# Block attention and an FFN in one kernel: PV on four array quadrants, DMA transposes of x, a new order of loads and work

## The chip, the cores and the metric

The kernel runs on one core of a Trainium2 chip. TensorE (PE) does matmuls into PSUM, VectorE (DVE) and ScalarE (ACT) work on PSUM and SBUF, GpSimd (POOL) and SyncE (SP) issue the DMAs here. The metric is the device time of one execution in microseconds (us); less is better.

## What is computed

Attention inside chunks of 64 tokens, then a feed-forward network (FFN) with a swish of its own slope per hidden column:

```python
B, H, S, D = 8, 8, 576, 64                       # q, k, v: fp32
scores = q_c @ k_c.T / sqrt(D)                   # per chunk of 64 tokens and head
attn   = exp(scores - max) / sum(...)
x      = (attn @ v_c) as [B * S, H * D]          # 4608 x 512
h      = x @ w_in                                # 512 -> 2048
g      = h / (1 + exp(-beta * h))
out    = g @ w_out                               # 2048 -> 512, fp32
```

## The kernel before

The 4,608 tokens are cut into 18 units of 256 tokens (four chunks, two tiles of 128). The FFN takes them in blocks: units 0 and 1 alone, then pairs (2, 3), (4, 5) and so on, ten blocks.

Attention of a unit has these steps. `load_qk` and `load_v` bring q, k and v from POOL's DMA queue, cast to fp16. `emit_T` transposes k and q on DVE in 32 x 32 blocks, four instructions. `emit_sc` does 64 small score matmuls (32 rows of contraction, accumulated over two halves `e`) into two PSUM tiles `sc0`, `sc1`; ACT takes the exponential into `et`. `emit_pv` is called once per tile of 128 tokens: 16 matmuls of 64 x 64 x 65, chunk `c` on partitions 64c of both input and output, so on two diagonal quadrants of the PE array; the 65th column of v is 1.0 and gives the sum. DVE divides (`rd`, then `x16`). `emit_xt` turns the tile on PE (four transposes into PSUM `xp`, which shares its buffer with `sc0`) and DVE copies it to `xt`.

The FFN of a block j: for each of 16 hidden groups m, `emit_m` does four matmuls into `hps` (contraction 512), ACT takes tanh into `sg`, DVE forms `gt` in fp16 (named stt below). `emit_t` does 16 matmuls for a tile of 128 tokens into `ops`, ACT copies to `osb`, SP's queue stores it. `hps` and `ops` rotate over four PSUM buffers.

Each engine runs its instructions in program order; nothing reorders them. That order is written out by hand: attention of the next block is taken in steps (`attn_step`), one ahead of each of the four `emit_t` of the block before (at m = 4), so a scoring step stands between two output tiles; the xt of the block's last tile stands directly ahead of its first `hps`. Loads come from POOL in the order unit 0, a quarter of `w_in`, unit 1, the rest of `w_in`, unit 2, all of `w_out`, unit 3; later units as attention advances. Eight POOL DMAs can be in flight.

Of the kernel before, what the change touches and what calls it, by code (L numbers as in the profile page):

```python
# [8 lines left out]
FP32 = mybir.dt.float32  # L9
FP16 = mybir.dt.float16  # L10
ACTF = mybir.ActivationFunctionType
ALU = mybir.AluOpType
# [3 lines left out]
def kernel(  # L16
# [10 lines left out]
    nc = tc.nc  # L27
# [3 lines left out]
    CH = 64  # L31
# [10 lines left out]
    qk_p = ctx.enter_context(tc.tile_pool(name="qk", bufs=5))  # L42
    qt_p = ctx.enter_context(tc.tile_pool(name="qt", bufs=2))
    et_p = ctx.enter_context(tc.tile_pool(name="et", bufs=3))
    rd_p = ctx.enter_context(tc.tile_pool(name="rd", bufs=3))
    x_p = ctx.enter_context(tc.tile_pool(name="x", bufs=3))
    gt_p = ctx.enter_context(tc.tile_pool(name="gt", bufs=2))
    sg_p = ctx.enter_context(tc.tile_pool(name="sg", bufs=3))
    osb_p = ctx.enter_context(tc.tile_pool(name="osb", bufs=3))
# [5 lines left out]
    beta_sb = const.tile([128, KFF], FP32)  # L55
    beta2_sb = const.tile([128, KFF], FP32)
    w_in16 = big.tile([128, KDM, DFF], FP16)
    w_out16 = big.tile([128, KFF, DM], FP16)
    vbig = big.tile([128, NTILE, H, VP], FP16)

    blocks = []
    u0 = 0
    for n in [1, 1] + [2] * ((NU - 2) // 2):
        blocks.append((u0, n))
        u0 += n
    NB = len(blocks)
    xt_t = {}
    unit_block = {}
    for j, (u0, n) in enumerate(blocks):
        xt_t[j] = big.tile([128, KDM, n * UNIT], FP16, name=f"xt{j}")  # L70
        for u in range(u0, u0 + n):
            unit_block[u] = (j, u - u0)
# [28 lines left out]

    def load_w_in(g):
        n = DFF // 4
        nc.gpsimd.dma_start(  # L104
            out=w_in16[:, :, g * n:(g + 1) * n],
            in_=moe_w_in[:, g * n:(g + 1) * n].rearrange("(k p) f -> p k f", p=128),
        )

    def load_w_out(g):
        n = KFF // 4  # L110
        nc.gpsimd.dma_start(  # L111
            out=w_out16[:, g * n:(g + 1) * n, :],
            in_=moe_w_out[g * n * 128:(g + 1) * n * 128, :].rearrange("(k p) f -> p k f", p=128),
        )
# [4 lines left out]
    def emit_T(u):  # L119
        for src, dst, nm in ((k_t, kT, "kT"), (q_t, qT, "qT")):  # L120
            a = src.pop(u)
            t = qt_p.tile([128, H, 2, 32, 2], FP16, tag=nm, name=nm)
            for r in range(2):
                nc.vector.transpose(  # L124
                    out=t[:, :, :, :, r],
                    in_=a[:, :, r, :].rearrange("p h (e i) -> p h e i", e=2),
                )
            dst[u] = t

    et_t = {}  # L130

    def emit_sc(u):
        qt, kt = qT.pop(u), kT.pop(u)
        sc = [ps_s.tile([128, H, CH], FP32, tag=f"sc{s}", name=f"sc{s}") for s in range(2)]
        for h in range(H):
            for e in range(2):
                for c in range(4):
                    p0, o0 = 32 * c, 64 * (c % 2)
                    nc.tensor.matmul(  # L139
                        out=sc[c // 2][o0:o0 + 64, h, :],  # L140
                        lhsT=kt[p0:p0 + 32, h, e].rearrange("p i r -> p (i r)"),
                        rhs=qt[p0:p0 + 32, h, e].rearrange("p i r -> p (i r)"),
                        start=(e == 0),
                        stop=(e == 1),
                    )
        for s in range(2):
            et = et_p.tile([128, H, CH], FP16, tag=f"et{s}", name=f"et{s}")
            nc.scalar.activation(out=et, in_=sc[s], func=ACTF.Exp, scale=scale)
            et_t[u, s] = et

    def emit_pv(u, s):
        i = 2 * u + s
        et = et_t.pop((u, s))
        x = ps_x.tile([128, 2, 4, 128], FP32, tag="x", name="x")
        for h in range(H):
            for c in range(2):
                p0 = 64 * c
                nc.tensor.matmul(  # L158
                    out=x[p0:p0 + 64, h // 4, h % 4, 0:D + 1],
                    lhsT=et[p0:p0 + 64, h, :],  # L160
                    rhs=vbig[p0:p0 + 64, i, h, 0:D + 1],
                )
        rd = rd_p.tile([128, 2, 4, 1], FP32, tag="rd", name="rd")
        nc.vector.reciprocal(out=rd, in_=x[:, :, :, D:D + 1])  # L164
        x16 = x_p.tile([128, 2, 4, D], FP16, tag="x16", name="x16")
        nc.vector.tensor_tensor(
            out=x16, in0=x[:, :, :, 0:D], in1=rd.to_broadcast([128, 2, 4, D]), op=ALU.mult
        )
        j, o = unit_block[u]
        t0 = o * UNIT + s * 128  # L170
        pend_x.append((j, t0, x16))

    pend_x = []

    def emit_xt():
        j, t0, x16 = pend_x.pop()
        xp = ps_s.tile([128, KDM, 128], FP16, tag="sc0", name="xp")
        xf = x16.rearrange("p a h d -> p (a h d)")
        for g in range(KDM):
            nc.tensor.transpose(out=xp[:, g, :], in_=xf[:, g * 128:(g + 1) * 128], identity=ident)  # L180
        nc.vector.tensor_copy(out=xt_t[j][:, :, t0:t0 + 128], in_=xp)  # L181
# [3 lines left out]
    def emit_m(j, m):  # L185
        n = blocks[j][1] * UNIT
        if m == 0:
            gt_t[j] = gt_p.tile([128, KFF, n], FP16, tag="gt", name="gt")
        hps = ps_p.tile([128, n], FP32, tag="p", name="hps")
        for kk in range(KDM):  # L190
            nc.tensor.matmul(  # L191
                out=hps,
                lhsT=w_in16[:, kk, m * 128:(m + 1) * 128],
                rhs=xt_t[j][:, kk, :],
                start=(kk == 0),
                stop=(kk == KDM - 1),
            )
        sg = sg_p.tile([128, n], FP32, tag="sg", name="sg")
        nc.scalar.activation(out=sg, in_=hps, func=ACTF.Tanh, scale=beta2_sb[:, m:m + 1])  # L199
        nc.vector.scalar_tensor_tensor(  # L200
            out=gt_t[j][:, m, :], in0=sg, scalar=1.0, in1=hps, op0=ALU.add, op1=ALU.mult
        )

    def emit_t(j, t):
        ops = ps_p.tile([128, DM], FP32, tag="p", name="ops")
        for kk in range(KFF):
            nc.tensor.matmul(  # L207
                out=ops,
                lhsT=gt_t[j][:, kk, t * 128:(t + 1) * 128],
                rhs=w_out16[:, kk, :],  # L210
                start=(kk == 0),
                stop=(kk == KFF - 1),
            )
        osb = osb_p.tile([128, DM], FP32, tag="osb", name="osb")
# [4 lines left out]
    attn = [[("sc", 0)], [("pv", 0, 0)]]  # L219
    for u in range(NU):  # L220
        attn.append(([("sc", u + 1)] if u + 1 < NU else []) + [("pv", u, 1)])
        if u + 1 < NU:
            attn.append([("pv", u + 1, 0)])
    attn.reverse()
    nxt_T = [0]
    nxt_load = [0]

    def loads_to(u):
        while nxt_load[0] <= min(u, NU - 1):
            w = nxt_load[0]  # L230
            load_qk(w)
            load_v(2 * w)
            load_v(2 * w + 1)
            nxt_load[0] += 1

    def attn_step():
        if pend_x:
            emit_xt()
        if not attn:
            return  # L240
        for op in attn.pop():
            if op[0] == "sc":
                emit_sc(op[1])
                if op[1] + 1 < NU:
                    emit_T(op[1] + 1)
                loads_to(op[1] + 4)
            else:
                emit_pv(op[1], op[2])

    with tc.manual_schedule():  # L250
        make_identity(nc, ident)
        nc.sync.dma_start(out=beta_sb, in_=moe_beta.rearrange("(k p) -> p k", p=128))
        nc.vector.memset(vbig[:, :, :, D:D + 1], 1.0)
        loads_to(0)
        load_w_in(0)
        loads_to(1)
        load_w_in(1)
        load_w_in(2)
        load_w_in(3)
        loads_to(2)  # L260
        load_w_out(0)
        load_w_out(1)
        load_w_out(2)
        load_w_out(3)
        loads_to(3)
        nc.scalar.activation(out=beta2_sb, in_=beta_sb, func=ACTF.Copy, scale=0.5)
        emit_T(0)
        for _ in range(3):
            attn_step()
        emit_xt()  # L270
        pend = []
        for j in range(NB):
            if pend_x:
                emit_xt()
            for m in range(KFF):
                if m == 4:
                    n_a = 4 if j else 2
                    for t in pend:
                        if n_a:
                            attn_step()  # L280
                            n_a -= 1
                        emit_t(j - 1, t)
                    pend = []
                if m in (4, 7, 10, 13) and n_a and (m > 4 or j == 0):
                    attn_step()
                    n_a -= 1
                emit_m(j, m)
            pend = list(range(2 * blocks[j][1]))
        for t in pend:
            emit_t(NB - 1, t)  # L290
# [30 lines left out]
```

## Time and profile before

| | |
|---|---|
| median of 3 runs | 357.28 us (354.85 to 357.56) |
| profiled execution: span from the first to the last instruction | 358.2 us |
| PE busy, share of the span | 297.4 us, 83% |
| DVE, ACT, POOL busy | 187.8, 144.6, 77.6 us |
| mean granted TensorE clock | 0.985 |
| read from HBM / written | 36.71 / 9.44 MB |

No other time is given for the profiled execution; its span stands for it. Busy times are sums over the whole span. Two stages with different limits are mixed in them, so the slices of the span and the chain of work that ended last tell more: the chain goes back from the last instruction, at each step to what released it.

### The profile page before, as it was taken

What the parts mean: (1) busy time and instruction counts of PE and PEld (TensorE: products, weight loads), DVE (VectorE), ACT (ScalarE), POOL (GpSimd) and SP (SyncE); (2) the same over time, 40 slices, a digit from 0 to 9 for tenths busy, and PEclk for the clock granted to TensorE, in tenths of its full rate; (3) what the DMA queues carried; (4) which work ended last, traced back from release to release, by engine and by line L of the source; (5) the groups of instructions that cost most, each with busy time, mean ns of one, the idle gap of its engine ahead of it and who ended that gap; (6) DMA issues with size and microseconds to landing.
All of it is one profiled execution on the core that took longest, in us unless ns stands there. A gap on an engine that the chain in (4) does not pass through costs nothing.

```text
span 358.2 us, 7186 instructions
## 1 busy us (share of the span) xinstructions
PE 297.4 (83%) x3088; PEld 154.6 (43%) x3088; DVE 187.8 (52%) x341; ACT 144.6 (40%) x234; POOL 77.6 (22%) x102
## 2 busy tenths in 40 slices
PE   0124669889889998999899989998999899899995
PEld 0122445644434543454355435443544354344442
DVE  1415566855856456745665565466547523730710
ACT  1111442642544256326622752274237324632821
POOL 9637389323230530053012000000000000000000
PEclk9999989989989999999999999999999999999999
DMA  9999999992990990099009000100100011001011
GB/s 98 188 193 187 184 170 182 194 110 43 107 88 31 128 136 4 31 148 119 2 31 148 29 0 31 60 31 0 56 36 31 2 60 59 0 31 59 29 44 75
DMA packets 86639, 28.25 MB, mean 79 GB/s; under 512 B 77904, under 2 KB 82000, under 8 KB 86608
## 3 DMA queue, kind: packets, MB, share of 16 engines
q0 software_dynamic: 79360, 18.36, 55.1%
q1 hardware_dynamic: 7248, 9.45, 7.5%
q8 instruction: 24, 0.39, 0.4%
q14 instruction: 7, 0.06, 0.0%
HBM read 36.71 MB, written 9.44 MB: 129 GB/s over the span
## 4 chain that ended last, share of the span: by engine, by line
PE 77%; DMA 8%; DVE 8%; POOL 4%; ACT 2%; issue 1%; POOLq 0%; ACTq 0%
PE ops L207 36%; PE hps L191 34%; DMA w_in_97<-in_moe_w_in_dram 4%; DMA ku<-in_k_dram 4%; PE x L158 3%; DVE gt L200 3%; ACT sg L199 2%; PE xp L180 1%; POOL vbig L97 1%; POOL w_out_98 L111 1%; POOL qu L89 1%; DVE kT L124 1%; DVE qT L124 1%; POOL w_in_97 L104 1%; POOL ku L89 0%
## 5 line engine op out<-in xcount | busy, mean ns | idle before, releaser
L200 DVE SCALAR_TENSOR_TENSOR gt<-sg,hps 128x512 f16<-128x512 f32 (+1 forms) x160 | 100.6, 633 | 82.1 <-ACT sg L199 82.0
L207 PE MATMUL ops<-w_out_98,gt 128*128 128x512 f16 x576 | 129.5, 380 | 0.0
L199 ACT ACTIVATE sg<-hps,beta_sb 128x512 f32<-128x512 f32 (+1 forms) x160 | 102.4, 645 | 65.1 <-PE hps L191 60.0
L191 PEld LDWEIGHTS <-w_in_97 128*128 128x128 f16 x640 | 64.5, 101 | 84.5 <-issue 25.1
L207 PEld LDWEIGHTS <-gt 128*128 128x128 f16 x576 | 54.1, 98 | 62.5
L215 ACT ACTIVATE osb<-ops 128x512 f32<-128x512 f32 x36 | 21.5, 597 | 110.9 <-PE ops L207 96.5
L89 POOL DMA_DIRECT2D qu<-in_q_dram x24 | 19.1, 799 | 98.5 <-DVE rd L164 93.2
L124 DVE STREAM_TRANSPOSE kT<-ku 128x512 f16<-128x512 f16 x36 | 24.2, 721 | 22.5 <-DMA ku<-in_k_dram 22.5
L97 POOL DMA_DIRECT2D vbig<-in_v_dram x40 | 34.0, 868 | 6.4 <-DMA w_in_97<-in_moe_w_in_dram 3.8
L124 DVE STREAM_TRANSPOSE qT<-qu 128x512 f16<-128x512 f16 x36 | 23.4, 699 | 0.0
L139 PEld LDWEIGHTS <-kT 32*64 32x64 f16 x1152 | 13.1, 110 | 22.1 <-issue 11.6
L89 POOL DMA_DIRECT2D ku<-in_k_dram x24 | 19.0, 796 | 4.8 <-DMA w_out_98<-in_moe_w_out_dram 3.8
L191 PE MATMUL hps<-xt_102,w_in_97 128*128 128x512 f16 x64 | 17.9, 443 | 1.1 <-DVE xt_102 L181 1.1
L191 PE MATMUL hps<-xt_106,w_in_97 128*128 128x512 f16 x64 | 14.1, 379 | 1.6 <-DVE xt_106 L181 1.6
L191 PE MATMUL hps<-xt_108,w_in_97 128*128 128x512 f16 x64 | 14.1, 379 | 1.6 <-DVE xt_108 L181 1.6
L191 PE MATMUL hps<-xt_103,w_in_97 128*128 128x512 f16 x64 | 14.1, 379 | 1.6 <-DVE xt_103 L181 1.6
L191 PE MATMUL hps<-xt_104,w_in_97 128*128 128x512 f16 x64 | 14.1, 379 | 1.6 <-DVE xt_104 L181 1.6
L191 PE MATMUL hps<-xt_105,w_in_97 128*128 128x512 f16 x64 | 14.1, 379 | 1.6 <-DVE xt_105 L181 1.6
L191 PE MATMUL hps<-xt_107,w_in_97 128*128 128x512 f16 x64 | 14.1, 379 | 1.6 <-DVE xt_107 L181 1.6
L191 PE MATMUL hps<-xt_109,w_in_97 128*128 128x512 f16 x64 | 14.1, 379 | 1.6 <-DVE xt_109 L181 1.6
L191 PE MATMUL hps<-xt_100,w_in_97 128*128 128x256 f16 x64 | 11.0, 345 | 4.7 <-DVE gt L200 4.2
L139 PE MATMUL sc_160<-qT,kT 32*64 32x64 f16 x32 | 1.1, 236 | 10.1 <-DVE qT L124 10.1
(274 smaller groups left out, 164.2 us busy)
## 6 DMA issues: line engine op xcount, KB each, us to landing
out_dram<-osb SPq DMA_DIRECT2D x36, 256.0 KB, 2.0
vbig<-in_v_dram POOLq DMA_DIRECT2D x32, 128.0 KB, 6.4
qu<-in_q_dram POOLq DMA_DIRECT2D x12, 256.0 KB, 5.2
ku<-in_k_dram POOLq DMA_DIRECT2D x12, 256.0 KB, 6.0
w_in_97<-in_moe_w_in_dram POOLq DMA_DIRECT2D x4, 512.0 KB, 10.9
w_out_98<-in_moe_w_out_dram POOLq DMA_DIRECT2D x4, 512.0 KB, 9.6
qu<-in_q_dram POOLq DMA_DIRECT2D x4, 192.0 KB, 5.5
ku<-in_k_dram POOLq DMA_DIRECT2D x4, 192.0 KB, 6.5
```

Source lines behind the costliest of these rows:

```text
L89: nc.gpsimd.dma_start(out=t[off // 2:(off + n) // 2], in_=src[b, :, s:s + n, :].rearrange("h (p r) d -> p h r d", r=2),)
L97: nc.gpsimd.dma_start(out=vbig[off:off + n, i, :, 0:D], in_=v[b, :, s:s + n, :].rearrange("h p d -> p h d"),)
L104: nc.gpsimd.dma_start(out=w_in16[:, :, g * n:(g + 1) * n], in_=moe_w_in[:, g * n:(g + 1) * n].rearrange("(k p) f -> p k f", p=128),)
L111: nc.gpsimd.dma_start(out=w_out16[:, g * n:(g + 1) * n, :], in_=moe_w_out[g * n * 128:(g + 1) * n * 128, :].rearrange("(k p) f -> p k f", ...
L124: nc.vector.transpose(out=t[:, :, :, :, r], in_=a[:, :, r, :].rearrange("p h (e i) -> p h e i", e=2),)
L139: nc.tensor.matmul(out=sc[c // 2][o0:o0 + 64, h, :], lhsT=kt[p0:p0 + 32, h, e].rearrange("p i r -> p (i r)"), rhs=qt[p0:p0 + 32, h, e].rea ...
L158: nc.tensor.matmul(out=x[p0:p0 + 64, h // 4, h % 4, 0:D + 1], lhsT=et[p0:p0 + 64, h, :], rhs=vbig[p0:p0 + 64, i, h, 0:D + 1],)
L191: nc.tensor.matmul(out=hps, lhsT=w_in16[:, kk, m * 128:(m + 1) * 128], rhs=xt_t[j][:, kk, :], start=(kk == 0), stop=(kk == KDM - 1),)
L199: nc.scalar.activation(out=sg, in_=hps, func=ACTF.Tanh, scale=beta2_sb[:, m:m + 1])
L200: nc.vector.scalar_tensor_tensor(out=gt_t[j][:, m, :], in0=sg, scalar=1.0, in1=hps, op0=ALU.add, op1=ALU.mult)
L207: nc.tensor.matmul(out=ops, lhsT=gt_t[j][:, kk, t * 128:(t + 1) * 128], rhs=w_out16[:, kk, :], start=(kk == 0), stop=(kk == KFF - 1),)
L215: nc.scalar.activation(out=osb, in_=ops, func=ACTF.Copy, scale=0.5)
```

## The change

PV of a unit becomes one step of 32 matmuls. The chunk picks the 64 input rows and now also the PSUM bank (`r`), heads 0 to 3 or 4 to 7 pick the 64 output partitions (`c`), so that all four quadrants of the array are used and heads h and h + 4 lie side by side. `emit_xt` and the FFN's first matmul are adapted to that layout: `xt` has 64-token pieces and the `hps` operand picks them.

q and k are transposed as 32-bit pairs, two DVE instructions a unit in place of four; the score matmuls then read their operands with a stride of two elements. Both score halves share one two-bank PSUM tile `s`, which the second PV tile also uses.

x of units 0 to 3 is still turned on PE (its `xp` now uses the FFN's PSUM buffers). From unit 4 on, a DMA transpose on SP's queue writes `xt`; SP waits there for the norm on DVE, with output stores behind it.

The first block is units 0 and 1, then 2 and 3 alone, then pairs. `w_in` comes in eight parts, all ahead of unit 2; three of the four `w_out` parts too. Block 0 does its first hidden groups in halves of 256 columns, and its output projection in four sweeps over k with all four `ops` tiles open. Later blocks place every step by a table of positions within the block. Matmuls on zeros (`emit_idle`) stand at the start. beta is loaded as rows and transposed on DVE.

```diff
-    for n in [1, 1] + [2] * ((NU - 2) // 2):
+    blocks = [(0, 2), (2, 1), (3, 1)] + [(u, 2) for u in range(4, NU, 2)]
...
     def emit_T(u):
...
-            t = qt_p.tile([128, H, 2, 32, 2], FP16, tag=nm, name=nm)
-            for r in range(2):
-                nc.vector.transpose(
-                    out=t[:, :, :, :, r],
-                    in_=a[:, :, r, :].rearrange("p h (e i) -> p h e i", e=2),
-                )
+            t = qt_p.tile([128, H, CH, 2], FP16, tag=nm, name=nm)
+            nc.vector.transpose(
+                out=t.rearrange("p h s e -> p (h s e)").bitcast(FP32).rearrange(
+                    "p (h i r) -> p h r i", h=H, r=2),
+                in_=a.rearrange("p h r d -> p (h r d)").bitcast(FP32).rearrange(
+                    "p (h r i) -> p h r i", h=H, r=2),
+            )
...
-    def emit_pv(u, s):
+    def emit_pv(u):
+        et = et_t.pop(u)
+        for s in range(2):
+            i = 2 * u + s
+            pool, tag = ((ps_x, "x"), (ps_s, "s"))[s]
+            x = pool.tile([128, 2, 4, 128], FP32, tag=tag, name="x")
+            for g in range(4):
+                for r in range(2):
+                    for c in range(2):
+                        nc.tensor.matmul(
+                            out=x[64 * c:64 * c + 64, r, g, 0:D + 1],
+                            lhsT=et[64 * r:64 * r + 64, s, 4 * c + g, :],
+                            rhs=vbig[64 * r:64 * r + 64, i, 4 * c + g, 0:D + 1],
+                        )
...
+    def emit_xt_dma(u, s):
+        xf = x16_t.pop((u, s)).rearrange("p r h d -> p (r h d)")
+        nc.sync.dma_start_transpose(out=xt_at(u, s), in_=xf)
...
-                rhs=xt_t[j][:, kk, :],
+                rhs=xr[:, c0 // CH:(c0 + n) // CH, 2 * (kk % 2) + kk // 2, :],
...
+        for s in range(4):
+            for t in range(4):
+                if s == 2 and t == 2:
+                    emit_T(2)
+                if s == 3 and t == 0:
+                    emit_sc(2)
+                if s == 3 and t == 2:
+                    emit_pv(2)
+                    emit_norm(2, 0)
+                    emit_norm(2, 1)
+                emit_t(0, t, 4 * s, 4 * s + 4)
+        emit_xt_pe(2, 0)
+        emit_xt_pe(2, 1)
+        emit_T(3)
...
+            items = [(m / KFF, 0, ("m", m)) for m in range(KFF)]
+            for t in range(nt):
+                for hf in range(2):
+                    items.append((0.18 + 0.8 * (t + 0.5 * hf) / nt, 1, ("t", t, hf)))
+            w = 0.86 / max(len(units), 1)
+            for i, u in enumerate(units):
+                a0 = 0.03 + i * w
+                items.append((a0, 2, ("sc", u)))
+                items.append((a0 + 0.40 * w, 3, ("pv", u)))
+                items.append((a0 + 0.41 * w, 3, ("norm", u, 0)))
+                items.append((a0 + 0.55 * w, 3, ("norm", u, 1)))
+                items.append((a0 + 0.70 * w, 3, ("T", u + 1)))
```

Three places in the instruction order. First PE, where the scores of a unit begin in the steady stage. Before, the transposes of x into `xp` stand between an output tile and the scores:

```order
L207 LDWEIGHTS gt
L207 MATMUL ops<-w_out_98,gt 128x512
L180 LDWEIGHTS x_1582
L180 MATMUL xp<-ident,x_1582 128x128
...
L139 LDWEIGHTS kT
L139 MATMUL sc_1610<-qT,kT 64x64
```

Now, in block 3, with `win_102` the first part of `w_in`:

```order
L207 LDWEIGHTS win_102
L207 MATMUL hps<-xt,win_102 128x512
L143 LDWEIGHTS kT
L143 MATMUL sc<-qT,kT 64x64
```

The scores follow a hidden group directly, and after their 64 matmuls the next hidden group follows, not PV.

Second DVE, over the end of a steady block and the next block's start, before:

```order
L200 SCALAR_TENSOR_TENSOR gt<-sg,hps 128x512 x12
L181 COPY xt_104<-xp 128x4x128
L200 SCALAR_TENSOR_TENSOR gt<-sg,hps 128x512 x4
L164 RECIPROCAL rd<-x 128x8
L166 TENSOR_TENSOR x_2066<-x,rd 128x512
L181 COPY xt_105<-xp 128x4x128
L124 STREAM_TRANSPOSE kT<-ku 128x512 x2
L124 STREAM_TRANSPOSE qT<-qu 128x512 x2
```

Now, one unit's share of a steady block:

```order
L216 SCALAR_TENSOR_TENSOR gt<-sg,hps 128x512 x5
L174 RECIPROCAL rd<-x 128x8
L176 TENSOR_TENSOR x_2342<-x,rd 128x512
L216 SCALAR_TENSOR_TENSOR gt<-sg,hps 128x512
L174 RECIPROCAL rd<-x 128x8
L176 TENSOR_TENSOR x_2366<-x,rd 128x512
L216 SCALAR_TENSOR_TENSOR gt<-sg,hps 128x512
L123 STREAM_TRANSPOSE kT<-ku 128x8x2x32
L123 STREAM_TRANSPOSE qT<-qu 128x8x2x32
```

The `xt` copies have left DVE, and the copy that stood behind twelve `gt` instructions at a block's end is gone.

Third SP, at the first units that are turned by DMA:

```order
L241 DMA out_dram<-osb 128x512 x4
L196 DMA_TRANSPOSE xt<-x_1295 128x4x128
L196 DMA_TRANSPOSE xt<-x_1309 128x4x128
L241 DMA out_dram<-osb 128x512
L196 DMA_TRANSPOSE xt<-x_1493 128x4x128
L196 DMA_TRANSPOSE xt<-x_1506 128x4x128
L241 DMA out_dram<-osb 128x512
```

Before, SP had only the 36 stores in a row after the load of beta; 28 transposes now stand between them.

More of the change, by code (lines that the diff above doesn't have):

```diff
@@ L236, in attn_step, with emit_idle @@
[L236 to L248, printed above, removed]
-    with tc.manual_schedule():
-        make_identity(nc, ident)
-        nc.sync.dma_start(out=beta_sb, in_=moe_beta.rearrange("(k p) -> p k", p=128))
+    def emit_idle(n, w):
+        d = ps_p.tile([128, 512], FP32, tag="p", name="warm")
+        for _ in range(n):
+            nc.tensor.matmul(out=d[:, 0:w], lhsT=idle[:, 0:128], rhs=idle[:, 0:w])
@@ L253, with loads_to @@
+    with tc.manual_schedule():
+        nxt = [0]
+        def loads_to(u):
+            while nxt[0] <= min(u, NU - 1):
+                load_unit(nxt[0])
+                nxt[0] += 1
+        nc.vector.memset(idle, 0.0)
+        nc.vector.memset(braw, 0.0)
         nc.vector.memset(vbig[:, :, :, D:D + 1], 1.0)
         loads_to(0)
[L255 removed]
+        make_identity(nc, ident)
         loads_to(1)
[L257 to L259 removed]
+        for g in range(8):
+            load_w_in(g)
+        for g in range(3):
+            load_w_out(g)
@@ L290 @@
+        for t in range(2 * blocks[NB - 1][1]):
             emit_t(NB - 1, t)
```

228 lines of the change are left out of this document (124 added, 104 removed).

## The prediction

> **What bounds the kernel now.** I read the busy table and the slices of the span first, to see which engine is full and when.
>
> ```profile
> span 358.2 us, 7186 instructions
> PE 297.4 (83%) x3088; PEld 154.6 (43%) x3088; DVE 187.8 (52%) x341; ACT 144.6 (40%) x234; POOL 77.6 (22%) x102
> PE   0124669889889998999899989998999899899995
> PEclk9999989989989999999999999999999999999999
> DMA  9999999992990990099009000100100011001011
> ```
>
> There are two stages. In the first eight or so slices (9 us each) the DMA engines are full and PE is not. After that PE is near 90% and nothing else is. So the later stage is priced by PE's own chain, the first one by what arrives when. Next I read the chain of work that ended last, in order of time, for one steady block of two units (columns: start, duration, what).
>
> ```profile
> 110.19 3.56 PE ops L207 x16
> 113.75 0.24 PE xp L180 x4
> 114.01 0.43 DVE xt_104 L181
> 114.48 0.21 PE sc_1610 L139 x2
> 115.19 0.37 PE x L158 x16
> 115.56 3.56 PE ops L207 x16
> 119.11 0.22 PE xp L180 x4
> 119.34 0.37 PE x L158 x16
> 119.71 3.56 PE ops L207 x16
> ...
> 125.08 3.56 PE ops L207 x16
> 128.64 10.37 PE hps L191 x48
> 139.03 0.69 ACT sg L199
> 139.75 0.69 DVE gt L200
> 140.44 0.35 DVE xt_104 L181
> 140.83 3.61 PE hps L191 x16
> 144.44 0.37 PE x L158 x16
> 144.81 3.56 PE ops L207 x16
> ```
>
> The pattern repeats from 110.19 to 144.81: 34.62 us. A dense 512-column matmul costs 10.37/48 = 0.216 us. A block needs 64 for `hps` and 64 for `ops`: 128 x 0.216 = 27.65 us. The other 6.97 us is attention, 3.5 us a unit. It stands in the rows: twice 1.81 us for transposing x, copying it, scoring and one PV step (113.75 to 115.56, and again before 125.08); 0.60 us for a transpose and a PV step (119.11); 1.82 us at the block's end, where PE waits for `xt` because its copy stands on DVE behind ACT's and DVE's last hidden-layer work (139.01 to 140.83); 0.37 us for the fourth PV step. The remaining 0.56 us is the tail of a group before a change of shape: 3.56 against 16 x 0.216 = 3.46, about 0.10 us each.
>
> **The steady stage, part by part.** From unit 4 on the PE transposes, their `xt` copies on DVE and the block-end wait go. What stays on PE per unit is one scoring and one PV step, each cut into the FFN.
>
> Scoring: the chain shows 0.71 us from the first score matmul (114.48) to PV (115.19). The instructions are the same 64; their operands are now read with a stride of two elements, which no row shows. It may gain nothing or cost double, and since fewer bytes per matmul do not move, I exclude a gain. I take 0.71 plus one group tail, 0.81; the upper end is 1.52.
>
> PV: two steps of 0.37 before. Now the 32 matmuls of a unit run in one go on four quadrants instead of two. If that doubles the overlap they take 0.37 and a tail, 0.47; if not, 0.84; a loss beyond that I exclude, since count, width and weights are the same. I take 0.54, near the lower end.
>
> So a unit costs 1.35 us (bounds 1.28 to 2.36) in place of 3.5. A steady block becomes 27.65 + 2.70 = 30.35 us, 4.3 less.
>
> What covers the rest: the exponential, the norm and the two 32-bit transposes of q and k run while PE does FFN groups placed between scoring and PV. A 32-bit transpose is not in the trace; by the rows below it is 0.67 us if it is paced by its 512 elements, 1.35 if by its bytes. Two per unit replace four. DVE is 52% busy over the span and gets less to do; either way it stays under PE, so this costs nothing here.
>
> The DMA transposes are the unknown. SP issues them, each behind a norm, between output stores. Its queue has room, but a unit's two transposes must land before the next block's first `hps`. The nearest rows, with queue totals (packets, MB, share) first:
>
> ```profile
> q0 software_dynamic: 79360, 18.36, 55.1%
> out_dram<-osb SPq DMA_DIRECT2D x36, 256.0 KB, 2.0
> beta_sb<-in_moe_beta_dram SPq DMA_DIRECT2D x1, 8.0 KB, 2.9
> ```
>
> A store of twice a transpose's 128 KB lands in 2.0 us. The `beta_sb` load, 2,048 single elements, lands in 2.9. At the far end, moving all 65,536 elements one packet each at the software queue's rate (79,360 packets in 55.1% of 358.2 us, 402 per us) would take 163 us. I take 2.9 us, the row nearest in kind. By the change's table the second unit's first norm stands at 0.03 + 0.43 + 0.41 x 0.43 = 0.636 of a block. That leaves 11.1 us of a 30.4 us block, 6.3 us of block 2 (17.2 us, below) and 8.5 us of block 3 (23.4 us). Two transposes in series, 5.8 us, fit in all three.
>
> **The start.** Rows of the start, from the chain and the timelines of DVE, ACT and PE (columns: start, duration, instruction, count, wait before it; one of them, an exponential, from the steady stage), then the window around the late stall and the groups for 256 columns:
>
> ```profile
> 0.76 0.19 POOL ident masks.py:197
> 1.44 1.01 POOL qu L89
> 7.49 1.35 DVE L124 STREAM_TRANSPOSE kT<-ku 128x512 f16<-128x512 f16 x2 [5.42 <-DMA ku<-in_k_dram]
> 15.09 1.35 DVE L124 STREAM_TRANSPOSE kT<-ku 128x512 f16<-128x512 f16 x2 [5.06 <-DMA ku<-in_k_dram]
> 17.54 0.17 DVE L164 RECIPROCAL rd<-x 128x8 f32<-128x8 f32 x1
> 17.74 0.69 DVE L166 TENSOR_TENSOR x_263<-x,rd 128x512 f16<-128x512 f32 x1
> 42.94 1.35 DVE L124 STREAM_TRANSPOSE kT<-ku 128x512 f16<-128x512 f16 x2 [3.48 <-DMA ku<-in_k_dram]
> 115.24 0.60 ACT L148 ACTIVATE et_1676<-sc_1610 128x512 f16<-128x512 f32 x1 [0.86 <-PE sc_1611 L139]
> 46.65 4.01 PE L191 MATMUL hps<-xt_100,w_in_97 128*128 128x256 f16 x20 [4.22 <-DVE gt L200]
> 45.00:54.00 9.00, 6.22 (x48) 4.61 (x49) 5.85 (x15) 4.19 (x10) 7.91 (x11) 0.81 2.05 170
> L199 ACT ACTIVATE sg<-hps,beta_sb 128x256 f32<-128x256 f32 x32 | 14.4, 474 | 22.3 <-PE hps L191 17.3 <-DVE gt L200 4.8
> L200 DVE SCALAR_TENSOR_TENSOR gt<-sg,hps 128x256 f16<-128x256 f32 x32 | 12.7, 418 | 8.7 <-ACT sg L199 8.6
> ```
>
> DVE works in order. At 42.94 its transpose of unit 3's k had waited for a load behind all weights; `gt` work stood behind it, and PE waited 4.22 us until 46.65, with the clock at 0.81 in that window. The change loads all weights but one part ahead of unit 2 and asks for unit 2 only inside block 0's output projection.
>
> Loading rate: between k of unit 0 (7.49) and of unit 1 (15.09) 1,280 KB landed, 168 KB per us. In the new order k0 lands 0.7 us sooner (no identity first: 0.76 to 1.44), at 6.8; k1 768 KB later, 11.4; the first `w_in` part (256 KB) at 14.4; one more every 1.52 us, the last at 25.1.
>
> Working it forward: two transposes (1.35) end at 8.15; scores (0.71) 8.9; two exponentials (0.60 each) 10.1, the second PV tile behind them. DVE's two norms (0.17 + 0.69 each) start after the first tile, near 9.9, and end at 11.6; a PE transpose and the last copy (0.24 + 0.43) 12.3; unit 1's transposes 13.6; its scores 14.3; the first `hps` with the first `w_in` part at 14.4. ACT does two exponentials and a tanh first, so DVE's first stt starts at 16.1; seven stt (0.42), two norms and two copies bring it to 21.6. The other 256 columns of these eight m are paced by ACT (0.474): 3.8 us, 25.4. Eight m at 512 columns, 32 x 0.216 = 6.9: 32.3. Output projection of four tiles, 64 x 0.216 = 13.8, with unit 2's attention at 1.35: 47.5. The last `w_out` part is needed from 43 us; with the same bytes ahead as before (k3 at 42.94, two loads later) it is there by 40.
>
> Then PE transposes and two copies, bare: 0.24 + 0.86 = 1.1 us, 48.6. Unit 3's transposes (1.35) stand on DVE ahead of block 1's `gt` and of scores 3: 49.9. Block 1 has 256-column m only and DVE sets its pace: 16 x 0.42 + two norms 1.72 + T(4) 1.35 = 9.8, 59.7; two copies 0.86, 60.6. Block 2: 16 m by ACT 7.6, two tiles 6.9, units 4 and 5 2.7, together 17.2: 77.8.
>
> **The sum.** Left at 77.8 are 14 units of FFN (64 x 0.216 = 13.83 each: 193.6), unit 3's output projection (6.9) and attention of 12 units (16.2), 216.7 in all: 294.5. The last rows of the chain show what follows the last matmul, to the span's end at 358.2:
>
> ```profile
> 340.52 13.83 PE ops L207 x64
> 354.42 0.60 ACT osb L215
> ```
>
> That is 3.8 us, unchanged: **298 us**. It is made against the profiled execution's span, 358.2; the median of the runs shown is 357.28, 0.3% less, and I leave that as it is. Of the 60 us, 26 come from 12 steady units at 3.5 - 1.35 = 2.15; the other 34 from the start, since 358.2 - 3.8 - 216.7 - 25.8 = 112 is when the kernel before has as much left.
>
> **Rivals.**
> (a) PE gains nothing from quadrants and pays for strided reads. Then 14 units (4 to 17) cost 2.36 each: 14 x 1.0 = +14, **312 us**. For it: no row shows either operand form. Against: the score matmuls already start 64 in 0.7 us, eleven ns apart, on several tiles, so reading is not obviously the limit.
> (b) Transposes land late. With T us each, two in series, the boundary waits are (2T - 6.3) + (2T - 8.5) + 5 x (2T - 11.1), each from zero up. At T = 6, midway between 2.9 and the 9.3 of (c), it is 5.7 + 3.5 + 4.5 = 13.7: **312 us**. For it: only SP's row-wise transfers are known; the 402 packets per us leave no room for element traffic. Against: 2.0 and 2.9 us above. The Trainium skill, VectorE: DVE Perf Modes, section The three transpose paths, gives 1309 ns for a 128x128 DMA transpose; four to a tile make an estimate of T = 5.2 us, so 4.1 + 1.9 and 304 us by it, and no run here shows one yet.
> (c) The same, far slower: from T = 9.3 us the waits reach 60 us and the kernel is **slower than 358**. At T = 10 it is 368. It takes SP or the DMA engines working nearly element by element.
> (d) The start stays bad: loads arrive later because 256-column parts move worse, or PE falls into the 0.81 clock between short bursts. Doubling the 7.2 us from the first `hps` to 21.6 and the 3.8 us after it gives **+11, 309 us**. For it: PE is half idle from 14 to 22 us. Against: no gap there nears the 4.22 us ahead of 46.65.
>
> **How the numbers follow.** Forecast 0.50, (a) 0.16, (b) 0.15, (d) 0.12, (c) 0.05, 0.02 for no visible change. Below the forecast lie the lower price of a unit (14 x 0.07 = 1) and a start whose DVE stretches overlap better: of the stretches that DVE paces to 21.6, 49.9 and 60.6, 18 us in all, some 7 could go. So 290 at the low end; at the high end (a) with (d) is 323, taken as 325, which leaves out only (c) and the far half of (b). A measurement of this kernel can tell about 1% from no change. Faster by over 1%: everything but (c) and the 0.02, less a little for what I have not seen: 0.92; within 1% 0.03; slower 0.05.
>
> **What would show it.** The chain should hold no `xp` and no `xt` after block 2, and steady blocks of 30.4 us. The first `hps` should start near 14.4, block 1 near 49, block 3 near 78. A DMA transpose should land in under 5.5 us; an idle PE ahead of the first `hps` of blocks 3 to 9 waiting for `xt` means (b). Scores above 1 us or PV above 0.8 per unit mean (a). I am wrong altogether if SP's transposes queue up, for then every block is paced by them.

## The result and the profile after

| | before | after |
|---|---|---|
| median of 4 runs each | 357.42 us (354.85 to 359.31) | 309.93 us (309.19 to 311.06) |
| ratio after / before | | 0.868, 95% interval 0.862 to 0.873 |
| span of the profiled execution | 358.2 us | 307.6 us (its time: 309.35 us) |

The time stands 1.75 us above the span, so the forecast of 298, made in spans, compares with 307.6: it was 9.6 us short. The page of the changed kernel, its busy table and slices of 7.7 us:

```profile
span 307.6 us, 7128 instructions
PE 285.0 (93%) x3034; PEld 142.4 (46%) x3034; DVE 153.6 (50%) x288; ACT 144.1 (47%) x226; POOL 80.6 (26%) x106
PE   6689998789569999999999999999999999999994
PEclk9779999999969999999999999999999999999999
DMA  9999999999999969959612121202120202001011
```

PE is full from the thirteenth slice on. The digits 5 and 6 in the eleventh and twelfth, at 77 to 92 us, are a hole that the forecast did not have, and it lies under full DMA digits. First the part that came as forecast, the chain over one steady block of two units:

```profile
142.76 0.64 PE sc L143 x64
...
147.83 0.38 PE x L164 x31
...
172.85 0.64 PE sc L143 x64
```

From the scores at 142.76 to the same ones of the next block at 172.85 it is 30.09 us (34.62 before). A unit's attention is one scoring of 0.64 and one PV of 0.38 us, and the chain holds PE work only.

Now the hole: the chain ahead of block 3, then PE's and SP's timelines there (start, duration, instruction, count, wait before it).

```profile
79.57 7.21 DMA xt<-x
...
86.91 1.86 PE hps L207 x4
88.78 1.00 PE sc L143 x34
89.77 2.21 PE hps L207 x8
```

```profile
79.37 1.47 PE L207 MATMUL hps<-xt,win 128*128 128x256 f16 x12
86.91 1.86 PE L207 MATMUL hps<-xt,win 128*128 128x512 f16 x4 [6.07 <-DMA xt<-x]
```

```profile
78.29 2.52 SPq L196 DMA_TRANSPOSE xt<-x  x2
```

Block 2 ends at 80.84 (79.37 + 1.47). Both transposes of unit 5 were issued between 78.29 and 80.81, and the last landed at 86.78. PE waited 6.07 us and then ran at half rate for about 5 us: four matmuls in 1.86 us that take 0.86 elsewhere. It is PE's only wait for `xt` by DMA in the trace. What a transpose does in this stretch and later, from the DMA view over 60 to 90 us and then over 140 to 300 us (the row of digits is the busy share of the 16 engines; the last number of a line is the median from issue to landing):

```profile
DMA  9999999999999999999999999999999999999999
...
out_dram<-osb SPq DMA_DIRECT2D x2, 256.0 KB, 7.3
...
xt<-x SPq DMA_TRANSPOSE x4, 7.1
```

```profile
out_dram<-osb SPq DMA_DIRECT2D x23, 256.0 KB, 2.1
...
xt<-x SPq DMA_TRANSPOSE x16, 2.3
```

The same transpose lands in 2.3 us when the engines are quiet and in 7.1 us while POOL's loads fill them. The output stores of the same queue go from 2.1 to 7.3 us with it. Both of these stand behind transposes in SP's queue, so they do not clear the transpose by themselves. Two earlier rows do: the changed kernel's four stores from 46.94 us on, issued before its first transpose (view of 45 to 60 us), and the first store of the kernel before, issued at 58.51 us (view of 0 to 60 us), where the median of all 36 is 2.0:

```profile
out_dram<-osb SPq DMA_DIRECT2D x4, 256.0 KB, 6.7
```

```profile
out_dram<-osb SPq DMA_DIRECT2D x1, 256.0 KB, 5.4
```

Plain stores are nearly as slow beside the loads, with no transpose ahead of them, so this is no property of the transpose; and the trace of the kernel before held a row with a price of that kind. By the Trainium skill (DMA: Bandwidth & Descriptors, section Queues, rings and completion order) each DMA engine takes turns between the queues that have work for it, packet by packet, and a completion is only signalled after all earlier writes of that engine, whatever their queue. Stores and transposes slowed alike agree with both halves of that; no run here tells them apart.

The start, from the chain, and one window of it (busy time of PE, PEld, DVE, ACT and POOL, then granted clock, DMA share, GB/s):

```profile
8.62 1.07 PE sc L143 x51
...
14.82 0.71 PE sc L143 x64
15.54 2.71 PE hps L207 x12
...
23.74 10.56 PE hps L207 x64
34.30 1.73 PE ops L229 x8
...
49.61 0.76 DVE xt L192 x2
50.37 0.62 DVE kT L123
50.98 0.60 DVE qT L123
...
51.63 0.71 PE sc L143 x64
...
53.34 0.47 ACT sg L215
...
53.83 0.43 DVE gt L216
...
63.64 0.60 PE hps L207 x4
```

```profile
8.00:16.00 8.00, 5.32 (x185) 4.43 (x186) 4.24 (x9) 1.49 (x3) 7.62 (x11) 0.75 1.84 180
```

Every milestone is 1 to 3 us late. Twelve 256-column matmuls take 2.71 us at 15.54, 0.226 us each, twice what 256 columns cost at full rate (half of 0.216). PE had been faster just before: the scores at 14.82 took 0.71 us, as the later ones at 51.63 do, where those at 8.62 took 1.07. Between the scores at 51.63 and block 2 at 63.64 the chain goes to and fro between ACT's `sg` and DVE's `gt`. PE's stall of 4.22 us that ended at 46.65 in the kernel before is gone.

### The profile page after: what moved, and what is told of

Read it like the earlier page. It is cut to its first block, busy times and chain, and to the rows that moved or that the text cites. A ratio compares the mean times of both kernels' runs of the same rounds, so it can differ in the third digit from the quotient of the medians.

```text
span 307.6 us, 7128 instructions
## 1 busy us (share of the span) xinstructions
PE 285.0 (93%) x3034; PEld 142.4 (46%) x3034; DVE 153.6 (50%) x288; ACT 144.1 (47%) x226; POOL 80.6 (26%) x106
## 4 chain that ended last, share of the span: by engine, by line
PE 85%; DVE 8%; DMA 4%; ACT 1%; issue 1%; POOL 0%; DVEq 0%; ACTq 0%; POOLq 0%
PE ops L229 40%; PE hps L207 39%; PE sc L143 4%; DVE gt L216 2%; DMA xt<-x 2%; PE x L164 2%; DVE x L176 2%; DMA ku<-in_k_dram 2%; ACT sg L215 1%; DVE kT L123 1%; DVE qT L123 1%; DVE xt L192 1%; DVE rd L174 0%; POOL qu L86 0%; PE warm L246 0%
## 5 line engine op out<-in xcount | busy, mean ns | idle before, releaser
L207 PE MATMUL hps<-xt,win 128*128 128x512 f16 (+1 forms) x672 | 141.7, 354 | 10.2 <-DMA xt<-x 6.1
L215 ACT ACTIVATE sg<-hps,beta 128x512 f32<-128x512 f32 (+1 forms) x168 | 104.0, 626 | 91.4 <-PE hps L207 87.2
L229 PE MATMUL ops<-wout,gt 128*128 128x512 f16 x576 | 134.2, 379 | 0.0
L207 PEld LDWEIGHTS <-win 128*128 128x128 f16 x672 | 64.3, 99 | 69.5 <-issue 11.9
L152 ACT ACTIVATE et<-sc 128x1024 f16<-128x1024 f32 (+1 forms) x20 | 18.6, 938 | 20.5 <-PE sc L143 20.5
L176 DVE TENSOR_TENSOR x<-x,rd 128x512 f16<-128x512 f32 x36 | 24.9, 692 | 1.2
L143 PE MATMUL sc<-qT,kT 32*64 32x64 f16 x1152 | 13.5, 197 | 5.7 <-DVE qT L123 5.7
L123 DVE STREAM_TRANSPOSE kT<-ku 128x512 f32<-128x512 f32 x18 | 12.7, 707 | 1.1 <-DMA ku<-in_k_dram 1.1
L123 DVE STREAM_TRANSPOSE qT<-qu 128x512 f32<-128x512 f32 x18 | 12.1, 671 | 0.0
L164 PE MATMUL x<-vbig,et 64*64 64x65 f16 x576 | 8.7, 200 | 0.1
```

The lines of the kernel that those rows point to most:

```text
L123: nc.vector.transpose(out=t.rearrange("p h s e -> p (h s e)").bitcast(FP32).rearrange("p (h i r) -> p h r i", h=H, r=2), in_=a.rearrange(" ...
L143: nc.tensor.matmul(out=sc[o0:o0 + 64, c // 2, h, :], lhsT=kt[p0:p0 + 32, h, :, e], rhs=qt[p0:p0 + 32, h, :, e], start=(e == 0), stop=(e == 1),
L152: nc.scalar.activation(out=et[:, s], in_=sc[:, s], func=ACTF.Exp, scale=scale)
L164: nc.tensor.matmul(out=x[64 * c:64 * c + 64, r, g, 0:D + 1], lhsT=et[64 * r:64 * r + 64, s, 4 * c + g, :], rhs=vbig[64 * r:64 * r + 64, i, ...
L176: nc.vector.tensor_tensor(out=x16, in0=x[:, :, :, 0:D], in1=rd.to_broadcast([128, 2, 4, D]), op=ALU.mult)
L207: nc.tensor.matmul(out=hps[:, 0:n], lhsT=w_in16[m // 2][:, kk, (m % 2) * 128:(m % 2) * 128 + 128], rhs=xr[:, c0 // CH:(c0 + n) // CH, 2 * ...
```

## The experiments

Two theories for the hole. **Theory 1:** the transposes land late because load traffic fills the DMA engines. **Theory 2:** something of their own delays them, such as their place in SP's queue or a late issue. Each kernel starts from the changed one; times are medians of four runs (five for two_quadrants), ratios against the kernel before on the same chip.

### unit5_by_pe and hold_loads: without the transposes, or without the loads

```diff
-                    if it[1] > 3:
+                    if it[1] > 3 and it[1] != 5:
                         emit_xt_dma(it[1], it[2])
...
+            if j == 2:
+                emit_xt_pe(5, 0)
+                emit_xt_pe(5, 1)
```

> The changed kernel, with only unit 5 turned on PE at the end of block 2 in place of the DMA transpose. Theory 1 and theory 2 agree that the wait for the DMA goes; what is left is a bare PE transpose and copy as ahead of block 2 (1.2 to 1.9 us). Block 3 should start near 83 instead of 86.9, with no slow clock behind: span 302 to 304. If it stays above 306, the wait ahead of block 3 was not the transposes' but the norm's.

304.77 us, ratio 0.849 (0.845 to 0.853), span 301.7. The chain at block 3's start:

```profile
81.84 0.68 DVE xt L192 x2
...
82.56 1.02 PE hps L207 x4
```

Block 3 starts 4.35 us earlier and at full rate. The price is PE's wait for DVE's two copies at the block's end. So the hole is unit 5's DMA transposes, and it costs 5 to 7 us net (5.2 by the medians, 6.7 by the ratios).

```diff
-                    loads_to(it[1] + 5)
+                    loads_to(7 if it[1] <= 5 else it[1] + 5)
```

> The changed kernel, with the loads of units 8 and later held until unit 6 is scored, so that no load should run while units 4 and 5 are transposed by DMA. Theory 1 (load traffic makes the transposes land late: 7.1 us there against 2.3 us later on): the four transposes of units 4 and 5 land in 2.3 to 3 us, PE's wait ahead of block 3 falls from 6.1 us to 1.3 or less, no slow clock after it, span 307.6 - 5 to - 7, about 301. Theory 2 (the norm simply comes too late; landing time does not depend on loads): wait and span unchanged within 1 us, landing still near 7 us. If the held loads are then missed by a later unit, a wait of DVE for ku appears in block 3 and eats the gain.

310.35 us, ratio 0.866 (0.862 to 0.870), span 308.5: no change, but the edit did not do what it was for. POOL's timeline still shows loads at the place that was to be quiet, and PE's wait is 6.2 us:

```profile
74.75 0.58 POOL L86 DMA_DIRECT2D ku<-in_k_dram  x1
...
78.14 0.68 POOL L94 DMA_DIRECT2D vbig<-in_v_dram  x1 [1.76 <-DMA qu<-in_q_dram]
```

POOL's program has nothing to wait for between blocks, so where a load is written beside PE's work does not set its time; free DMAs and buffers do. The run tells nothing about the theories.

### qk_five_buffers and qk_four_buffers: loads held back by what they do wait for

```diff
-    qk_p = ctx.enter_context(tc.tile_pool(name="qk", bufs=7))
+    qk_p = ctx.enter_context(tc.tile_pool(name="qk", bufs=5))
```

> The changed kernel with five q and k buffers in place of seven. GpSimd's queue runs ahead of the other engines as far as its buffers go; the attempt before this one, which only moved the load instructions in program order, left the loads beside the transposes. With five buffers the load of unit 10 has to wait for unit 5's transposes (about 72 us) and that of unit 11 for unit 6's (about 81 us), so that the DMA engines should be idle near 77 to 81 us, where unit 5 is transposed. Theory 1 (load traffic makes the transposes land late): landing falls from 7.1 us to 2.3 to 4 us, PE's wait ahead of block 3 from 6.1 us to 1 to 3, span 301 to 304. Theory 2 (late norm only): landing and wait unchanged, span 307 to 309.

The other kernel has `bufs=4` there. (The kernel before the change had five.)

> The buffers of the raw k and q loads are cut to four each, so the loads of units 9 and 10 can only be issued when the units whose buffers they take have been normed, and the DMA engines should be quiet when the transposes of unit 5 are issued (about 78 to 81 us). Theory 1 (the transposes land late because load traffic fills the 16 DMA engines): landing of unit 5's second transpose pair 2.3 to 3 us, PE's wait ahead of block 3 at most 1.3 us, span 301 to 303 us, time 304 to 306. Theory 2 (the transposes of this unit are slow for another reason, such as their place in SP's queue or the first use of the path): landing 5 us or more and span 307 to 309 as with five buffers. A risk for both: a later load is now late and VectorE waits for it, which would show as a DMA wait of ku or qu.

307.67 us, ratio 0.860 (0.853 to 0.867), with five; 306.79 us, ratio 0.860 (0.855 to 0.865), with four. The DMA row over 74 to 88 us and PE's wait, for five and then for four buffers (with seven the row is all nines and the wait 6.07):

```profile
DMA  9999689992759999999999999999541111999999
...
87.28 1.02 PE L207 MATMUL hps<-xt,win 128*128 128x512 f16 x4 [3.77 <-DMA xt<-x]
...
88.95 3.45 PE L207 MATMUL hps<-xt,win 128*128 128x512 f16 x8
```

```profile
DMA  7805949469999999999999999199964969999999
...
84.46 1.02 PE L207 MATMUL hps<-xt,win 128*128 128x512 f16 x4 [2.05 <-DMA xt<-x]
```

The longest landing in the trace falls from 8.7 us (seven buffers) to 5.8 and 4.1, the wait from 6.07 to 3.77 and 2.05, with the transposes and SP's queue untouched. That is theory 1 by its direction. It misses its numbers: at most 4 us of landing were expected with five buffers and 3 with four, but loads of other units were still under way, as the nines in both rows show. With five buffers block 3 even begins 0.37 us later than with seven (87.28 against 86.91), though PE waits 2.3 us less. Block 2 began 1.2 us later there (64.86), and its first work and the eight matmuls at 88.95 ran at about half rate (3.45 us, 1.9 at full rate). In the profiled executions a slow start of block 2 also stands in unit5_pe_early_T3, where the buffers are untouched (its scores at 64.37 take 1.07 us), so it isn't put down to the buffers. The spans, 303.6 to 308.0 with five and 303.5 to 306.2 with four over four runs, bear the order out weakly.

### earlier_unit5 and earlier_unit5_four_buffers: more lead

```diff
-            w = 0.86 / max(len(units), 1)
+            w = (0.66 if j == 2 else 0.86) / max(len(units), 1)
```

> Only the table of positions of block 2 changes: each of its two units takes 0.33 of the block instead of 0.43, so the norm of unit 5, behind which its DMA transposes are issued, stands at 0.495 instead of 0.636 of the block, by position 2.4 us earlier. The loads are untouched. Theory 1 (the landing is long because of the loads, and the short lead adds to it): landing stays near 7 us, PE's wait ahead of block 3 falls from 6.1 us by the lead gained, to 3 to 4.5 us, span 304.5 to 306.5. Theory 2 (the lead alone was wrong, a transpose issued earlier lands as quickly as the later ones): the wait goes, span 301 to 302.5. Rival (the block is paced by VectorE, earlier attention work costs as much ahead of the block's end): span 307 to 309.

310.64 us, ratio 0.867 (0.860 to 0.874), span 308.9. PE's timeline in block 2 and at its end, and DVE's second norm of unit 5:

```profile
73.03 0.71 PE L143 MATMUL sc<-qT,kT 32*64 32x64 f16 x64 [2.53 <-DVE qT L123]
87.37 1.86 PE L207 MATMUL hps<-xt,win 128*128 128x512 f16 x4 [3.49 <-DMA xt<-x]
```

```profile
78.79 0.69 DVE L176 TENSOR_TENSOR x<-x,rd 128x512 f16<-128x512 f32 x1
```

The wait fell by 2.58 us, into theory 1's range, but not by its mechanism. The norm came at 78.79, where it had come at 78.74, and the last transpose landed at 87.23, where it had landed at 86.78: no lead was gained. Block 2 ended 3.0 us later instead (83.87), since it began 0.9 us later and 2.53 us of waiting for DVE's q transpose appeared ahead of the scores (0.62 before). So the rival holds: attention in block 2 is paced by DVE and ACT, and a smaller number in the table moves PE's order without moving the norm.

> The earlier norm of unit 5 as in earlier_unit5 and four buffers each for raw k and q as in qk_four_buffers. Theory 1: with about 2 us left of the wait by the buffers alone, the added lead takes it to 0.5 us or less; block 3 starts by 83 us, span 300.5 to 302.5, time 302.5 to 304.5. If the two are one effect (a lead that only shifts the transposes back into load traffic), the wait stays at 2 us and the span at 303.5 to 305.

305.90 us, ratio 0.854 (0.849 to 0.859), span 302.9. The chain at block 3's start:

```profile
82.62 2.17 PE hps L207 x16
```

The first twelve matmuls of this row are block 2's, the last four, at 0.86 us, are block 3's first: it follows without a gap at 82.62 + 1.31 = 83.93, and no wait for a DMA's `xt` is left, as expected. Block 3's start (83 expected), span (at most 302.5) and time (at most 304.5) all come out higher: block 2 itself began at 64.59 instead of 63.64, and the 2.53 us of waiting for DVE are in this run too. The norm was not earlier here either (78.84). Landings of 4.0 us or less and a later end of block 2 closed the gap together, so the run is no proof that more lead helps.

### two_quadrants: PV on two quadrants again

```diff
-                            out=x[64 * c:64 * c + 64, r, g, 0:D + 1],
+                            out=x[64 * r:64 * r + 64, c, g, 0:D + 1],
```

The operand of `hps` is adapted to it.

> The changed kernel with PV back on the two diagonal quadrants (chunk c on partitions 64c of input and output, x laid out as before the change, the FFN's operand read accordingly), still 32 matmuls in one step. If four quadrants double the overlap, as the forecast took it (0.37 us against 0.74 per unit): PV steps of 0.74 us from first matmul to the next group, 18 x 0.37 = 6.7 us more, of which the 13 in the steady stage at least, 4.8, show in the span: 312 to 315. Rival (the step is limited by issue, not by quadrants): PV stays at 0.38 us, span 307.6 within 1.

314.22 us, ratio 0.876 (0.871 to 0.880). The chain's PV in a steady block:

```profile
153.99 0.63 PE x L164 x32
```

0.63 against 0.38 us: 0.25 us for each of 18 units are 4.5 us, and the medians differ by 4.3; by the ratios it is 2.9 us, with intervals that overlap, so the rows carry this finding and the times only agree with it. Four quadrants make PV 1.66 times as fast as two, not twice.

### early_T2: unit 2's transposes ahead of block 0's hidden layer

```diff
         emit_sc(1, True)
+        emit_T(2)
...
-                if s == 2 and t == 2:
-                    emit_T(2)
```

> The changed kernel with unit 2's q and k transposes moved on DVE from the output projection of block 0 to just behind the scores of unit 1, where an in-order DVE must wait for loads that stand behind all of w_in and three parts of w_out. Theory (what the start gained is the end of such in-order stalls): DVE waits from about 15 to 36 us, PE runs out of PSUM buffers after a few hidden groups, the hidden groups start over near 36 with a cold clock, span +14 to +18, about 323. Rival (the start is bound by the arrival of the weights anyway): w_in is complete by 25 us, so no more than +8, about 315.

322.76 us, ratio 0.901 (0.896 to 0.907). DVE's timeline:

```profile
35.80 0.71 DVE L123 STREAM_TRANSPOSE kT<-ku 128x512 f32<-128x512 f32 x1 [20.89 <-DMA ku<-in_k_dram]
```

The `gt` work stood behind that wait for 20.89 us, and block 0's long stretch of `hps` began at 42.15 instead of 23.74. The kernel got 12.8 us slower than the changed one from moving two instructions. The place where the change puts them is worth that.

### all_by_pe: no DMA transposes at all

```diff
+                if u > 3:
+                    items.append((a0 + 0.85 * w, 3, ("xt", u, 0)))
+                    items.append((a0 + 0.95 * w, 3, ("xt", u, 1)))
...
-                    if it[1] > 3:
-                        emit_xt_dma(it[1], it[2])
```

> The changed kernel without DMA transposes: units 4 to 17 are turned on PE too, each tile as a step of its own behind the unit's last step, copied by DVE. In the steady stage each unit should pay two groups of four transposes on PE, 0.24 us and a tail of 0.1 each, 0.7 us a unit: blocks of 31.5 us in place of 30.1, 14 units 9.5 us more. The 6.1 us wait ahead of block 3 and the slow clock behind it (some 2 us) go. Together 307.6 + 9.5 - 8 = 309. Rival (transposes on PE are hidden, the wait before the change was only a matter of their place): blocks of 30.1 to 30.4 us and a span near 300.

314.85 us, ratio 0.881 (0.876 to 0.885). One steady block in the chain:

```profile
151.79 0.22 PE xp L191 x4
...
152.87 0.22 PE xp L191 x4
153.10 0.64 PE sc L143 x64
...
185.28 0.64 PE sc L143 x63
```

The span, 313.2 us, is 4 us above the 309 that were expected, and a block takes 32.18 us in place of 30.09 (31.5 expected): two groups of PE transposes of 0.22 a unit, the rest PE's waits for `gt` (7.6 us over the span, in ten places). Against unit5_by_pe the DMA transposes of the other 13 units save 10 us.

### no_idle_matmuls: the matmuls on zeros left out

All three `emit_idle` calls go.

> The changed kernel without the 26 matmuls on zeros at the start. If they hold up the granted clock, scores, PV and the first hidden groups run at half speed: the first hps later by 1 us at most, the groups up to 34 us slower, span +1 to +4. Rival (the start is paced by loads, DVE and ACT up to 34 us): span within 1 us of 307.6.

311.80 us, ratio 0.871 (0.865 to 0.877): not to be told from the changed kernel's 0.862 to 0.873. From its chain and its windows:

```profile
15.00 1.07 PE sc L143 x37
16.06 2.67 PE hps L207 x12
```

```profile
8.00:16.00 8.00, 4.17 (x169) 3.26 (x169) 4.20 (x9) 1.09 (x2) 7.63 (x11) 1.00 1.83 180
```

The first hidden group is 0.5 us later and as slow as with the zeros. With them the scores ahead of it ran faster (0.71 us at 14.82, here 1.07), but the rate was lost again by 15.54. Nor is it sure to come: in earlier_unit5_four_buffers, with the same start, those scores took 1.07 us too. The clock column reads 1.00 here and 0.75 with the zeros, though no row is faster here: it shows what the records hold, and a matmul's own duration tells the rate.

### unit5_pe_early_T3 and xt_inside_blocks: two tries for a faster version

To unit5_by_pe the first adds unit 3's transposes right after unit 2's scores:

```diff
                     emit_sc(2)
+                    emit_T(3)
...
-        emit_T(3)
```

> Unit 5 on PE as in the run with that name (301.7 us), and unit 3's q and k transposes moved on DVE ahead of unit 2's norms, into the time from 37 to 47 us in which DVE is idle. If k of unit 3 has landed by 46 us, block 1 starts without the 1.3 us of DVE work in front of its gt and scores: span 1 to 2 us less, about 300. If it lands later, DVE waits in order, unit 2's norms come late and block 1 starts late: span 302 to 306.

304.59 us, ratio 0.851 (0.846 to 0.856): unit5_by_pe's time. Unit 3's k landed early enough (DVE's transpose of it began at 43.21), and block 1's first `hps` came 1.0 us earlier than in unit5_by_pe (51.22 against 52.25). But block 2 began no earlier (63.76 against 63.55), so the 1 to 2 us that were expected did not come.

The second keeps that and places the PE transposes of units 3 and 5 inside their blocks:

```diff
+            w = (0.72 if j == 2 else 0.86) / max(len(units), 1)
...
+            if j in (1, 2):
+                p = 3 if j == 1 else 5
+                items += [(0.80, 4, ("xt", p, 0)), (0.86, 4, ("xt", p, 1))]
...
-            if j == 1:
-                emit_xt_pe(3, 0)
-                emit_xt_pe(3, 1)
```

> Unit 5 goes through PE transposes and unit 3's raw tiles are prepared right after the scoring of unit 1, as in unit5_pe_early_T3; in addition the PE transposes of units 3 and 5 are placed inside blocks 1 and 2 (at 0.80 and 0.86 of the block) instead of behind them, and block 2's steps are packed earlier. Theory 1 (blocks 2 and 3 begin late only because PE waits 1.2 to 1.7 us at the block's end for VectorE's copies of the transposes): these two waits go, span 299 to 301 us, time 301 to 303. Rival (VectorE paces these blocks, and work placed earlier only moves the wait into the block): span within 1 us of unit5_pe_early_T3, time 304 to 305, with the waits now inside the block.

305.16 us, ratio 0.854 (0.850 to 0.858), where 301 to 303 were expected. Its chain at the starts of blocks 3 and 4:

```profile
81.22 1.02 PE hps L207 x4
...
101.78 4.38 DMA xt<-x
...
106.21 1.04 PE hps L207 x4
```

Block 3 begins 3.05 us earlier than in unit5_pe_early_T3 (84.27), but block 4 only 1.4 (106.21 against 107.61): unit 7's transposes, now issued earlier beside loads, land late, and PE waits 1.66 us for them. The wait moved one block on. unit5_by_pe, 304.8 us, stays the simplest of the versions that beat both kernels; four of them lie within 1.4 us of each other, and these runs don't rank them.

## Why the prediction was right or wrong

It was right on the sign, the size class and the steady stage, and short by 9.6 us of span. By its own steps (the forecast's sum is 298.3, given as 298):

| start of | forecast us | measured us | added to the miss |
|---|---|---|---|
| first `hps` | 14.4 | 15.54 | 1.1 |
| long stretch of block 0's `hps` | 21.6 | 23.74 | 1.0 |
| its output projection | 32.3 | 34.30 | -0.1 |
| scores of unit 3 | 49.9 | 51.63 | -0.3 |
| block 2 | 60.6 | 63.64 | 1.3 |
| block 3 | 77.8 | 86.91 | 6.1 |
| from there to the end, with the tail | 220.5 | 220.69 | 0.2 |

- **The steady block** (30.35 forecast, 30.09 measured). Strided operands cost nothing: 64 scores take 0.64 us inside the stream, less than the 0.71 assumed, and 0.71 behind a wait (51.63), as before the change. PV takes 0.38, the lower end. With tails a unit is (30.09 - 27.65) / 2 = 1.22 us, just below my lower bound of 1.28. Rival (a) is refuted, though two_quadrants shows that doubling the quadrants does not halve the time.
- **The 32-bit transposes** on DVE take 0.62 and 0.60 us in the chain: paced by elements, as taken.
- **The step that failed is the landing of the DMA transposes.** I took T = 2.9 us from rows of single transfers, without asking what else was on the DMA engines at 78 us, although the row of the kernel before read 9 there and its first store, under such digits, took 5.4 us. With T = 5.4 the forecast's own formula gives a first wait of 4.5 us instead of none. Quiet, T is 2.3; beside the loads it was 7.0 to 8.7. The second half of the step failed as well. I gave them 6.3 us of block 2 by the norm's place in the table, and the first issue came 2.55 us before the block's end (78.29 to 80.84), because DVE and ACT set the norm's time and not the table (earlier_unit5). A third part was wrong in my favour: two transposes are issued 1.3 us apart and overlap, so 2T in series was too much. With a quiet 2.3 us and the true lead the second would land near 79.57 + 2.3 = 81.9, and the wait would be about 1 us; the other 5 are load traffic.
- **Rival (b)** named this mechanism with 312 us. It was half of what happened: one wait at block 3, as large as its first term at T = 6 (5.7), and none at the six later boundaries, because the loads end and T falls to 2.3. The estimate of 5.2 us from the Trainium skill (VectorE: DVE Perf Modes, section The three transpose paths) is borne out neither by the quiet 2.3 nor by the busy 7.1. Rival (c) did not occur.
- **Rival (d)**, the start, came with 3.0 us instead of 11: PE at half rate for the first scores (8.62) and again for the first hidden group (15.54 to 18.25), with scores at full rate between, and block 1 slower by 1.3 us than my count of DVE's work alone, where the chain alternates between ACT and DVE. What would keep PE at full rate through the first hidden group stays open: with the zeros and without them it was as slow.
- **What was left** came out even: the half rate after the hole cost about 1.7 us (1.86, 1.00 and 2.21 against 0.86, 0.64 and 1.83), and six steady blocks at 0.26 less gave 1.6 back.

So the sum's mechanism held where the profile was quiet, and the miss is one term, priced from the wrong part of the trace.

## What to carry to other kernels

Price a transfer from rows that run under the same DMA load as the place where it will stand: here a small transfer took three times as long beside a saturated load queue, and it hung on the critical path once. Turn the data of the units whose transposes fall into the load stage on another engine, or bound the prefetch by buffers. A position in a hand-written order is not a time: neither POOL's loads nor DVE's norm moved with it, and the wait turned up at the next place.

## What the runs showed of the hardware that was not expected

- PE does not lose its full rate at a fixed point of a gap. After 3.49 us of waiting (earlier_unit5) the first four matmuls took 1.86 us. After 3.77 us (qk_five_buffers) they took 1.02, and the loss came behind the scores that follow, in the eight matmuls at 88.95. After 2.05 us (qk_four_buffers) there was none: the eight in that place took 1.90. By the Trainium skill (TensorE: Matmul & The Clock Gate, section What's actually happening) the clock gate watches a free-running window of about 3.4 us, so where the loss falls would depend on how the windows lie to the gap; these rows agree with that.
- A DMA transpose of 128x512 fp16 occupies SP's queue for 1.19 us and lands in 2.3 us on quiet engines, hardly more than a plain 256 KB store (2.1).
- 32 PV matmuls on four quadrants take 0.38 us, on two 0.63: 12 and 20 ns each.
